# Agent attention with a gated convolution: VectorE subtracts the last low halves, the last chunk is split 384 and 128, and eleven places of TensorE's written order are moved

## The chip, the cores and the metric

The kernel runs on one core of a Trainium2 chip. Its engines work side by side, each through a queue of its own that is done in order: TensorE (PE in the profile) for matrix products, VectorE (DVE), ScalarE (ACT) and GpSimd (POOL) for work on elements, and SyncE (SP), which here issues almost all DMA transfers. The metric is the time of one execution on the device in microseconds (us).

## The reference

Two stages follow each other. Agent attention takes q, k, v of 4 batches x 12800 rows x 128 columns through 49 agents, and its output is the input of a gated convolution with 5 taps:

```python
    a2k = sm(agents, k)
    agent_v = a2k @ v
    q2a = sm(q, agents)
    x = q2a @ agent_v
    for k in range(K):
        gate_pre += conv_w[k][None, None, :] * xp[:, k:k + S, :]
    gate = 1.0 / (1.0 + np.exp(-gate_pre))
    val = x @ w_val
    return (gate * val @ w_out)
```

## The kernel before

**Tiling.** A batch is worked in 10 units of 1280 rows for k, v and q (loads of 640 KB into a ring of 11 slots, `ld`), and in 25 chunks of 512 rows for the gated convolution. A chunk's number t runs over all batches, 0 to 98; the last 512 rows are cut into two chunks, 99 and 100, of 256 rows each (`CUT = 2`). Two units make a segment of 2560 rows, five chunks.

**Stages.** The steps of TensorE have short names, used in the written order and in this document. `k b.u` and `q b.u` are the score products of batch b and unit u (L376), `v b.u` the product of the agents' weights with v (L480), `m` the two small transposes for the maximum of k, `f` the five steps that fold the agents' values with the weights into `stat` and `wo16` (L522 to L728). The softmax of q (the agents' weights for each row) goes over VectorE, GpSimd and ScalarE and ends in a tile `pt`; `t b.u` transposes it into `x1`: by TensorE for the first four units (L849), by a DMA transpose on SP's queue for all others (L835, `x<-pt` in the profile). When both units of a segment have landed, two DMAs copy shifted rows from `x1` into `x2` (L884, `x<-x`), and GpSimd copies a halo of 4 columns for the next segment (L819). Then for each chunk `g t` is the gate's product (five matmuls on `x1`, L922, and a sixth on `x2`, L926), `a t` the value's (L949, L953) and `o t` the output's (L992 to L994).

**A chunk between its products.** ScalarE takes tanh of the gate (`th`), VectorE makes h = (th + 1) * val (L962), ScalarE casts h to f16, the high half `hh` (L968), GpSimd subtracts, `hl` = h - hh (L973), the low half. The output is hh and hl times the folded weights; ScalarE evicts it into `ob` (L1006) and SP sends it out (L1021), two chunks at a time, the last ones of a batch alone.

**What sets the order.** Every step is handed to a planner (`Plan.add`) with the engine, a time in us, and what it reads and writes. TensorE keeps the order in which the steps were written: that is the string `order` in the kernel, with one word for each step. For all other engines and for SP's queue the planner works out an order from the given times: of the steps that could start, it takes the one with the longest work behind it (`Plan.order`). So a word moved in the string, or another time in an `add`, can also move steps on ScalarE, VectorE, GpSimd and SP. Loads are handed over up to 11 ahead of the step that uses them. In the trace, SP waits with whatever stands at the head of its queue, and what is behind it waits too.

Of the kernel before, what the change touches and what calls it, by code (L numbers as in the profile page):

```python
# [13 lines left out]
ALU = mybir.AluOpType  # L14
# [12 lines left out]
CH = 512  # L27
# [12 lines left out]
NT_, NH = 3, 3  # L40
NPT = 4
NX = 4
CUT = 2
NOB = 4
LEAD = 5
MAX_AT = (7, 8)
# [21 lines left out]
class Plan:  # L68
# [11 lines left out]
    def add(self, engine, us, fn, reads=(), writes=(), moved=0.0, key=None, urge=0.0):  # L80
        i = len(self.steps)
        need = set()
        for x in reads:
            need |= self.wrote.get(x, set())
        for x in writes:
            need |= self.wrote.get(x, set()) | self.read.get(x, set())
        for x in reads:
            self.read.setdefault(x, set()).add(i)
        for x in writes:
            self.wrote[x], self.read[x] = {i}, set()  # L90
        self.steps.append((engine, us, fn, need, moved, key))
        self.urge.append(urge)
# [84 lines left out]
def tile_agent_attention_gated_conv(  # L177
# [9 lines left out]
    nc = tc.nc  # L187
    B, C, N = qT.shape
# [3 lines left out]
    NT = B * NCH  # L192
# [56 lines left out]
    def bank():  # L249
# [16 lines left out]
        out=fold, in0=ident[:, 0:AP_], in1=ident[:, AP_:P], op=ALU.add  # L266
# [625 lines left out]


    chunks = [(t // NCH, t % NCH * CH, CH) for t in range(NT - 1)]
    chunks += [(B - 1, N - CH + i * CH // CUT, CH // CUT) for i in range(CUT)]
    banks = {}

    def gates(t):
# [43 lines left out]
    def values(t):  # L942
        b, n0, w = chunks[t]
        stat, x2, o2, xs, x2k, st, th = state.pop(t)
        pv, at_v = banks[t][2:]
        scale = w / CH

        def matmuls():
            nc.tensor.matmul(  # L949
                out=pv, lhsT=stat[:, TAPS, :], rhs=x1s[(b * NCH + n0 // CH) // 5 % NX][:, PAD + o2 : PAD + o2 + w],  # L950
                start=True, stop=False,
            )
            nc.tensor.matmul(  # L953
                out=pv, lhsT=stat[0 : TAPS * X2R, TAPS + 2, :],
                rhs=x2[0 : TAPS * X2R, o2 : o2 + w], start=False, stop=True,
            )

        h, hh, hl = hs[t % NH][:, 0:w], hhs[t % 3][:, 0:w], hls[t % 3][:, 0:w]
        add("pe", 0.43 * scale, matmuls, xs + x2k + st, [at_v], key="c")
        add(  # L960
            "dve", 0.13 + 0.53 * scale,
            lambda: nc.vector.scalar_tensor_tensor(  # L962
                out=h, in0=th, scalar=1.0, in1=pv, op0=ALU.add, op1=ALU.mult
            ),
            [at_v, ("th", t % NT_)], [("h", t % NH)],
        )
        add(
            "act", 0.16 + 0.42 * scale, lambda: nc.scalar.copy(out=hh, in_=h),  # L968
            [("h", t % NH)], [("hh", t % 3)],
        )  # L970
        add(
            "pool", 0.1 + 1.07 * scale,
            lambda: nc.gpsimd.tensor_tensor(out=hl, in0=h, in1=hh, op=ALU.subtract),  # L973
            [("h", t % NH), ("hh", t % 3)], [("hl", t % 3)],
        )

# [80 lines left out]
    for b in range(B):  # L1057
        t0 = b * NCH
# [19 lines left out]
    for t in range(len(chunks) + 2):  # L1078
# [8 lines left out]
    kinds = {"m": "max", "f": "fold"}  # L1087
    order = (
# [25 lines left out]
    )  # L1114
    first = [(kinds.get(x[0], x[0]), *map(int, x[1:].split("."))) for x in order.split()]
    for w in first:
# [5 lines left out]
    def gate_and_state(t):  # L1122
# [3 lines left out]
        "k": key_scores, "v": agent_values, "q": queries, "t": transposes,  # L1126
        "max": lambda b: step(key_max, b), "fold": lambda b: step(fold_weights, b),
        "g": gate_and_state, "a": values, "o": project,
    }
    ahead, done = 0, 0  # L1130
# [56 lines left out]
```

## Time and profile before

| | |
|---|---|
| median of 3 runs (lowest, highest) | 427.45 us (425.69, 428.92) |
| the profiled execution | 425.66 us |
| its span, first to last instruction | 423.6 us |
| mean granted clock of TensorE | 0.985 |
| DMA, all packets | 127.62 MB, mean 301 GB/s |

The times are of one core. The profile is one execution: busy time is what an engine works, and a number in square brackets is the idle time of the engine just before the instruction, with what ended it. In the chain of waits each row is a piece of the chain that ended last, with its start and its length; a DMA's piece runs from its issue to its landing. `PEclk` is the share of full speed that was granted to TensorE's clock, and the DMA share is the busy time of the 16 DMA engines over the stretch, where 1.0 is all of them; it can pass 1.0 because packets of one engine overlap.

### The profile page before, as it was taken

To read this page: it belongs to the slowest core of one execution; us is meant where nothing else is said; L and a number is where in the kernel's file an instruction comes from. 1 tells how busy PE (TensorE), PEld (TensorE's weight loads), DVE (VectorE), ACT (ScalarE), POOL (GpSimd) and SP (SyncE) were. 2 spreads that over 40 slices of the span, in tenths; PEclk is the share of its full clock that TensorE was granted. 3 is DMA by queue.
4 is the path that set the end of the run, shared out by engine and by line. 5 is a ranking of instruction groups with operands and counts; after the bars stand their busy time and mean duration, and the time that the engine had idled before them with its cause. 6 is when DMAs were issued, how large, how long until landed. Compare 5 with 4: busy or idle time off the path is not lost.

```text
span 423.6 us, 10042 instructions
## 1 busy us (share of the span) xinstructions
PE 403.9 (95%) x3907; PEld 197.0 (47%) x3907; DVE 293.3 (69%) x562; ACT 301.5 (71%) x521; POOL 228.2 (54%) x263
## 2 busy tenths in 40 slices
PE   4979999999999999999999899999999989999995
PEld 1358434346555443446555343335555534344443
DVE  3757899867875978667795575767765678676231
ACT  1564568779966777678876486778876567788776
POOL 1002557654657565554566355574366277877553
PEclk9969999999999999999999899999999999999998
DMA  8999999999999999999999999999999977755733
GB/s 320 420 417 411 370 367 353 301 295 310 412 293 283 346 317 362 304 278 356 351 379 324 271 299 370 314 332 302 296 393 322 239 196 161 199 163 176 205 121 124
DMA packets 75129, 127.62 MB, mean 301 GB/s; under 512 B 50466, under 2 KB 50850, under 8 KB 75084
## 3 DMA queue, kind: packets, MB, share of 16 engines
q1 hardware_dynamic: 74940, 126.87, 96.9%
q8 instruction: 30, 0.49, 0.5%
q10 hardware_dynamic: 144, 0.13, 0.2%
q14 instruction: 15, 0.12, 0.1%
HBM read 79.25 MB, written 26.21 MB: 249 GB/s over the span
## 4 chain that ended last, share of the span: by engine, by line
PE 78%; DMA 9%; DVE 8%; ACT 1%; POOL 1%; issue 1%; SPq 0%; POOLq 0%; DVEq 0%; ACTq 0%
PE gate L922 23%; PE sc L376 17%; PE av L480 10%; PE val L949 5%; PE out L992 5%; PE val L953 5%; PE gate L926 5%; PE out L993 4%; DMA ld<-kT 4%; PE out L994 4%; DMA x<-pt 3%; DMA x<-x 2%; DVE h L962 1%; DVE qw L772 1%; DVE qsm L763 1%
## 5 line engine op out<-in xcount | busy, mean ns | idle before, releaser
L973 POOL TENSOR_TENSOR hl<-h,hh 128x512 f16<-128x512 f32 (+1 forms) x101 | 116.9, 1158 | 96.1 <-ACT hh L968 96.0
L922 PE MATMUL gate<-x,stat 128*128 128x512 f16 (+1 forms) x500 | 125.2, 380 | 0.2 <-ACT th L935 0.2
L962 DVE SCALAR_TENSOR_TENSOR h<-th,val 128x512 f32<-128x512 f32 x100 | 67.8, 678 | 66.8 <-PE out L993 26.2
L376 PE MATMUL sc<-ld,ag_sb 128*32 128x320 f32 x1280 | 101.5, 447 | 7.6 <-DMA ld<-kT 7.0
L935 ACT ACTIVATE th<-gate,unscale 128x512 f32<-128x512 f32 x100 | 68.3, 683 | 33.3 <-PE gate L926 31.7
L1006 ACT ACTIVATE ob<-out,oscale 128x512 f32<-128x512 f32 x98 | 67.3, 687 | 21.3 <-PE out L994 20.1
L922 PEld LDWEIGHTS <-stat 128*128 128x128 f16 x505 | 46.3, 97 | 63.7 <-issue 14.8
L968 ACT CAST hh<-h 128x512 f16<-128x512 f32 (+1 forms) x101 | 61.5, 609 | 17.2 <-DVE h L962 16.4
L750 POOL TENSOR_TENSOR qw<-sT,qmx 128x490 f32<-128x490 f32 x40 | 41.4, 1035 | 47.6 <-DVE qmx L745 47.5
L376 PEld LDWEIGHTS sc<-ld,ag_sb 128*32 128x32 f32 x1280 | 36.7, 111 | 59.4 <-issue 25.7
L480 PE MATMUL av<-ld,eT 128*32 128x129 f32 (+1 forms) x1400 | 50.7, 279 | 1.0 <-DVE eT L386 1.0
L480 PEld LDWEIGHTS av<-ld,eT 128*32 128x32 f32 (+1 forms) x1400 | 47.1, 117 | 7.5 <-issue 2.5
L794 POOL TENSOR_TENSOR pt<-qw,pt 128x490 f16<-128x490 f32 x40 | 44.8, 1120 | 3.1 <-ACT pt L779 2.9
L471 ACT ACTIVATE e<-ks,kbias 128x320 f32<-128x320 f32 x80 | 39.3, 554 | 5.4 <-DVE eT L386 3.3
L386 DVE STREAM_TRANSPOSE sT<-sc 128x640 f32<-128x640 f32 x40 | 33.6, 839 | 13.4 <-PE sc L376 12.7
L402 ACT COPY ks<-sc 128x640 f32<-128x640 f32 x40 | 27.7, 691 | 21.2 <-PE sc L376 19.1
L386 DVE STREAM_TRANSPOSE eT<-e 128x640 f32<-128x640 f32 x40 | 33.5, 842 | 9.8 <-ACT e L471 5.2
L926 PE MATMUL gate<-x,stat 95*128 95x512 f16 x100 | 38.3, 383 | 1.5 <-DMA x<-x 1.5
L949 PE MATMUL val<-x,stat 128*128 128x512 f16 x100 | 38.2, 382 | 0.8 <-DVE h L962 0.6
L953 PE MATMUL val<-x,stat 95*128 95x512 f16 x100 | 38.1, 381 | 0.0
L994 PE MATMUL out<-hl,wo 128*128 128x512 f16 x98 | 37.0, 378 | 1.1 <-POOL hl L973 1.1
L992 PE MATMUL out<-hh,wo 128*128 128x512 f16 x98 | 37.3, 381 | 0.1
(130 smaller groups left out, 389.4 us busy)
## 6 DMA issues: line engine op xcount, KB each, us to landing
ld<-kT SPq DMA_DIRECT2D x40, 640.0 KB
ld<-qT SPq DMA_DIRECT2D x40, 640.0 KB
ld<-vP SPq DMA_DIRECT2D x39, 645.0 KB
outT<-ob SPq DMA_DIRECT2D x48, 512.0 KB
x<-x SPq DMA_DIRECT2D x18, 375.0 KB
x<-x SPq DMA_DIRECT2D x18, 100.0 KB
outT<-ob SPq DMA_DIRECT2D x3, 256.0 KB
x<-x SPq DMA_DIRECT2D x4, 187.5 KB
```

Of the source, the lines that this page charges most:

```text
L376: nc.tensor.matmul(out=out[g * BLK : (g + 1) * BLK, j, 0:GT], lhsT=ag_sb[:, b, j * BLK : (j + 1) * BLK], rhs=src[:, g * GT : (g + 1) * GT] ...
L386: nc.vector.transpose(out=out.rearrange("p n (j i) -> p j n i", j=2), in_=in_.rearrange("p j (n i) -> p j n i", i=BLK),)
L480: nc.tensor.matmul(out=av[o + j : o + j + cols, 0 : C + 1], lhsT=et[:, n, j : j + cols], rhs=vt[:, n, :], start=(u == 0 and n < 2), stop=( ...
L922: nc.tensor.matmul(out=pg, lhsT=stat[:, k, :], rhs=x1[:, c : c + w], start=(k == 0), stop=False,)
L926: nc.tensor.matmul(out=pg, lhsT=stat[0 : TAPS * X2R, TAPS + 1, :], rhs=x2[0 : TAPS * X2R, o2 : o2 + w], start=False, stop=True,)
L935: lambda: nc.scalar.activation(out=th, in_=pg, func=AF.Tanh, scale=unscale[:, 0:1]),
L949: nc.tensor.matmul(out=pv, lhsT=stat[:, TAPS, :], rhs=x1s[(b * NCH + n0 // CH) // 5 % NX][:, PAD + o2 : PAD + o2 + w], start=True, stop=False,
L953: nc.tensor.matmul(out=pv, lhsT=stat[0 : TAPS * X2R, TAPS + 2, :], rhs=x2[0 : TAPS * X2R, o2 : o2 + w], start=False, stop=True,)
L962: lambda: nc.vector.scalar_tensor_tensor(out=h, in0=th, scalar=1.0, in1=pv, op0=ALU.add, op1=ALU.mult),
L968: "act", 0.16 + 0.42 * scale, lambda: nc.scalar.copy(out=hh, in_=h),
L973: lambda: nc.gpsimd.tensor_tensor(out=hl, in0=h, in1=hh, op=ALU.subtract),
L1006: lambda: nc.scalar.activation(out=ob[:, o : o + w], in_=po, func=AF.Copy, scale=oscale),
```

## The change

It has three parts. The last 512 rows are cut into 384 and 128 instead of 256 and 256. For the two chunks made of them (t of 99 and 100) the low half is subtracted by VectorE (0.53 us for 512 columns in the planner's table, where GpSimd has 1.07). And in TensorE's written order eleven places are moved: in the first fold the steps `f0`; `q0.6`, `q1.4`, `q2.1` and `q2.8` with `k3.8` to an earlier place, `o44` ahead of the fold `f2`, `k3.2` and `k3.3` behind `o48`, `t2.5` later, `t3.0` earlier, `a72` ahead of `o70`, and in the tail `o96` ahead of `a98`. What is computed stays the same.

```diff
-CUT = 2
+CUTS = (384, 128)
...
-    chunks += [(B - 1, N - CH + i * CH // CUT, CH // CUT) for i in range(CUT)]
+    chunks += [(B - 1, N - sum(CUTS[i:]), w) for i, w in enumerate(CUTS)]
...
-        add(
-            "pool", 0.1 + 1.07 * scale,
-            lambda: nc.gpsimd.tensor_tensor(out=hl, in0=h, in1=hh, op=ALU.subtract),
+        on, eng, us = (nc.vector, "dve", 0.53) if t >= NT - 1 else (nc.gpsimd, "pool", 1.07)
+        add(
+            eng, 0.1 + us * scale,
+            lambda: on.tensor_tensor(out=hl, in0=h, in1=hh, op=ALU.subtract),
...
-        "v0.5 v0.6 v0.7 v0.8 v0.9 f0 t0.0 f0 q0.1 k1.0 f0 k1.1 f0 q0.2 g0 k1.2 f0 t0.1 a0 q0.3 "
+        "v0.5 v0.6 v0.7 v0.8 v0.9 f0 t0.0 q0.1 k1.0 f0 k1.1 f0 f0 q0.2 g0 k1.2 f0 t0.1 a0 q0.3 "
...
-        "o95 g98 a98 o96 g99 o97 a99 g100 a100 o98 o99 o100"
+        "o95 g98 o96 a98 g99 o97 a99 g100 a100 o98 o99 o100"
```

Three queues show what follows from it. The first is SP's, at the transposes of units 1.8 and 1.9 (pt_99 and pt_100), which chunk 45 needs; pt_97 is unit 2.0, x_105 the shifted rows of chunk 45. Before:

```order
L835 DMA_TRANSPOSE x_1_102<-pt_99 128x10x128
L369 DMA ld_71<-kT 128x1280
L835 DMA_TRANSPOSE x_1_102<-pt_100 128x10x128
L1021 DMA outT<-ob_123 128x1024
L369 DMA ld_61<-kT 128x1280
L369 DMA ld_62<-qT 128x1280
L884 DMA x_105<-x_1_102 75x1x2560
```

After:

```order
L835 DMA_TRANSPOSE x_1_102<-pt_99 128x10x128
L369 DMA ld_71<-qT 128x1280
L369 DMA ld_61<-kT 128x1280
L835 DMA_TRANSPOSE x_1_102<-pt_100 128x10x128
L1023 DMA outT<-ob_123 128x1024
L369 DMA ld_62<-kT 128x1280
L835 DMA_TRANSPOSE x_2_103<-pt_97 128x10x128
L884 DMA x_105<-x_1_102 75x1x2560
```

The load of q and one of k now stand ahead of the second transpose, and the transpose of unit 2.0 ahead of the shift.

The second is TensorE's, in the first fold. L564 is the second of its steps `f0`, L659 the third, L376 are score products (of q0.1 on sc_135 and ld_71, k1.0 on ld_61, k1.1 on ld_62), and the row of L849 is the last of `t0.0`. Before:

```order
L849 MATMUL sc_134<-ident_143,pt_97 128x128
L564 MATMUL val<-avT,moe_sb 128x49
L376 MATMUL sc_135<-ld_71,ag_sb 32x320 x8
L376 MATMUL sc_134<-ld_61,ag_sb 32x320 x8
L659 LDWEIGHTS wst_124
```

After:

```order
L849 MATMUL sc_134<-ident_143,pt_97 128x128
L376 MATMUL sc_135<-ld_71,ag_sb 32x320 x8
L376 MATMUL sc_134<-ld_61,ag_sb 32x320 x8
L564 MATMUL val<-avT,moe_sb 128x49
L376 MATMUL sc_135<-ld_62,ag_sb 32x320 x8
L659 LDWEIGHTS wst_124
```

The second step of the fold moved behind two score products, the third behind three.

The third is ScalarE's at the end: casts (hh), tanh (th) and evictions (ob) from chunk 98 on. Before:

```order
L968 CAST hh_116<-h_113 128x512
L935 ACTIVATE th_108<-gate,unscale_131 128x256
L1006 ACTIVATE ob_122<-out,oscale_133 128x512
L968 CAST hh_114<-h_111 128x256
L935 ACTIVATE th_109<-sc_135,unscale_131 128x256
L1006 ACTIVATE ob_122<-sc_134,oscale_133 128x512
L968 CAST hh_115<-h_112 128x256
```

After:

```order
L968 CAST hh_116<-h_113 128x512
L935 ACTIVATE th_108<-gate,unscale_131 128x384
L1008 ACTIVATE ob_122<-out,oscale_133 128x512
L935 ACTIVATE th_109<-sc_135,unscale_131 128x128
L968 CAST hh_114<-h_111 128x384
L968 CAST hh_115<-h_112 128x128
L1008 ACTIVATE ob_122<-sc_134,oscale_133 128x512
```

The tanh of chunk 100 and both casts of the last two chunks moved ahead of the eviction of chunk 98 (ob_122<-sc_134). Behind the last h on VectorE stand two subtractions (128x384 and 128x128) that stood at the end of GpSimd's queue, with 256 columns each.

18 rows, old and new, of the table order are left out of this document.

## The prediction

> **What bounds the kernel now.** I read the page first: who is busy, and when.
>
> ```profile
> PE 403.9 (95%) x3907; PEld 197.0 (47%) x3907; DVE 293.3 (69%) x562; ACT 301.5 (71%) x521; POOL 228.2 (54%) x263
> ...
> DMA  8999999999999999999999999999999977755733
> ```
>
> TensorE is busy for 95% of the span, but the DMA engines stand at 9 up to slice 32 of 40 (some 339 us). So there may be two bounds, one after the other. The table by stretches says where each holds:
>
> ```profile
> core 0: us, PE busy (x), PEclk, DMA share, GB/s
> 200.00:236.00 36.00, 34.51 (x470) 1.00 1.09 337
> 236.00:339.00 103.00, 102.99 (x1031) 0.98 1.09 319
> 339.00:347.00 8.00, 6.31 (x45) 1.00 0.93 213
> 347.00:424.00 77.00, 72.06 (x395) 0.98 0.57 163
> ```
>
> Up to 339 us both are full: the DMA share is 1.09 and TensorE works 102.99 of 103 us. After 347 the share falls to 0.57 and TensorE alone is left. So I next looked at TensorE's timeline for the places behind 200 us where it waits for something:
>
> ```profile
> 235.67 0.39 PE L926 MATMUL gate<-x,stat 95*128 95x512 f16 x1 [1.50 <-DMA x<-x]
> ...
> 340.13 0.38 PE L994 MATMUL out<-hl,wo 128*128 128x512 f16 x1 [1.11 <-POOL hl L973]
> ...
> 346.25 0.38 PE L949 MATMUL val<-x,stat 128*128 128x512 f16 x1 [0.58 <-DVE h L962]
> ```
>
> These are gate 45 (1.50 us), output 69 (1.11) and value 73 (0.58). The chain of waits names what is behind them:
>
> ```profile
> 220.73 7.50 DMA x<-pt
> ...
> 228.28 7.34 DMA x<-x
> ...
> 331.87 6.86 DMA x<-pt
> ...
> 338.78 0.19 POOL x L819
> 338.97 2.23 POOL hl L973 x2
> 341.20 0.57 POOL gw L541
> ...
> 341.79 0.47 DVE wst L607
> ...
> 346.25 0.38 PE val L949
> ```
>
> Gate 45 waits for a shift that lands at 228.28 + 7.34 = 235.62. The other two have one cause: the transpose of unit 3.1 lands at 331.87 + 6.86 = 338.73; GpSimd's halo copy waits for it, and behind that copy stand the low halves of chunks 69 and 70 and the fold's gw, which VectorE needs before its weights and before h of chunk 72. So value 73 at 346.25 hangs on the landing at 338.73, not on when TensorE arrives. TensorE could come 1.11 + 0.58 = 1.69 us later without moving it, and if it came earlier it would wait longer. **The end is the landing of transpose 3.1 plus 346.25 - 338.73 = 7.52 us plus TensorE's work behind value 73.** What is saved ahead of 338 us without making the DMA queue shorter is lost again there. The profiled execution took 425.66 us (span 423.6); the median of the runs is 427.45, so 1.79 is added at the end.
>
> **The change part by part.**
>
> *SP's queue at chunk 45.* The planner has reordered it, as the rows in the part on the change show. One load now stands ahead of transpose 1.9, and transpose 2.0 ahead of the shift. The load was ahead of the shift already; transpose 2.0 is new there.
>
> ```profile
> 212.77 7.23 SPq L835 DMA_TRANSPOSE x<-pt  x1
> ...
> 225.49 0.73 SPq L369 DMA_DIRECT2D ld<-qT  x1
> ...
> 228.28 1.65 SPq L884 DMA_DIRECT2D x<-x  x2
> 230.04 5.71 SPq L835 DMA_TRANSPOSE x<-pt  x2
> ...
> L835 SPq DMA_TRANSPOSE x<-pt x36: 1352/3061/7234, 73.3 to 392.5; - x36
> ```
>
> The trace has no such order, so I bound it. A transpose holds SP for 1.35 us at the least, 3.06 at the median, 7.23 at the most. One load of the queue takes 1.59, the spacing of the first key products, each of which waits for its load:
>
> ```profile
> 18.63 1.28 PE L376 MATMUL sc<-ld,ag_sb 128*32 128x320 f32 x16 [0.30 <-DMA ld<-kT]
> 20.22 1.28 PE L376 MATMUL sc<-ld,ag_sb 128*32 128x320 f32 x16 [0.30 <-DMA ld<-kT]
> ```
>
> With the median, SP comes to transpose 2.0 a load later than it came to q 2.5: 225.49 + 1.59 = 227.1, and is done at 230.1, so the shift is issued 1.9 us later. By the queue alone it lands 1.35 later. I take 1.6, between these two; the ends are 0 (all of it beside loads in flight) and 6.0 (an issue of 7.23). Gate 45 then starts at some 237.3. Those 1.6 us are hidden by the 1.69 us of cover at chunks 69 and 73; of a shift that is later than that, the rest would come through.
>
> *The half clock behind that wait* is there before and after, so it adds nothing here:
>
> ```profile
> 233.57:236.98 3.41, 1.91 (x11) 1.02 (x10) 1.10 (x4) 1.43 (x3) 0.53 (x1) 1.00 1.26 190
> 236.98:240.40 3.42, 3.42 (x9) 1.18 (x9) 2.01 (x7) 1.30 (x2) 1.84 (x3) 0.50 1.05 335
> ```
>
> In the first window TensorE worked 1.91 of 3.41 us, and for the next 3.42 us the granted clock was 0.50, which costs 1.7 us of work. The Trainium skill (TensorE: Matmul & The Clock Gate, section "What's actually happening") wants one idle window of about 3.4 us before the clock is halved; here a wait of 1.50 us was enough, so the measurement decides. By the page's rule the wait of 3.1 us forecast here would leave the clock full and bring TensorE to chunk 69 earlier by 1.7 us, to wait there; the sum is the same, but the slow rival below would be 1.7 us milder.
>
> *The first fold.* On TensorE, f0's second product (L564) now stands behind q0.1 and k1.0, and only k1.1 lies between it and the transposes of the weights (L659).
>
> ```profile
> 42.38 0.42 PE L564 MATMUL val<-avT,moe_sb 128*128 128x49 f32 x2
> ...
> 45.03 0.79 PE L659 MATMUL gate<-ident,wst 128*128 128x128 f16 x8
> ...
> 52.07 0.72 PE L849 MATMUL sc<-ident,pt 128*128 128x128 f16 x10 [0.52 <-DVE sT L386]
> ...
> 43.40 0.20 DVE L588 TENSOR_REDUCE mx<-val 128x1 f32<-128x49 f32 x1
> 44.33 0.53 DVE L582 SCALAR_TENSOR_TENSOR wst<-val,rs,wst 128x30 f16<-128x30 f32 x3
> ```
>
> VectorE's weights run 43.40 to 44.86, 1.46 us; they start some 1.6 us later now (behind sT and qmx of q 0.1), and one product of 1.1 us covers less than two did: up to 0.75 us of new wait ahead of L659. Against it q 0.1's softmax comes earlier and the 0.52 us ahead of L849 goes. Net 0, ends -0.5 to +0.75; either way gate 45 takes it in, where TensorE waits 1.50 us now.
>
> *The other moves* (q0.6, q1.4, q2.1, o44, k3.2, k3.3, t2.5, q2.8, t3.0, a72) lie where the DMA share is 1.09. q2.1, o44 and k3.2 pass steps that TensorE does without a gap, so the same work is done in another order: 0. a72 ahead of o70 brings nothing, since value 73 waits for h of chunk 72, and VectorE's order there is unchanged.
>
> *The queue's length up to transpose 3.1.* SP has the same 217 DMAs ahead of it, before and after. Only SP's holds differ. Shift and transpose 2.1 no longer leave SP 5.71 us in two transposes in a row: a gain of at most 5.71 - 2 x 1.35 = 3.0. Transpose 2.7 moves behind three more DMAs, and while SP then waits for its landing one load instead of three DMAs is queued: a loss of at most 2 x 1.59 = 3.2. I take 0, ends -3.0 and +3.2, which is the widest term.
>
> GpSimd's halo copy waits for transpose 2.7 too, with chunk 60's low half behind it:
>
> ```profile
> 298.82 0.19 POOL L819 COPY x<-x 128x4 f16<-128x4 f16 x1 [2.58 <-DMA x<-pt]
> ...
> 299.94 1.16 POOL L973 TENSOR_TENSOR hl<-h,hh 128x512 f16<-128x512 f32 x1
> ...
> 305.95 0.38 PE L994 MATMUL out<-hl,wo 128*128 128x512 f16 x1
> ```
>
> It comes three DMAs later, at most 3 x 1.59 = 4.8 us, at 303.6, and the low half ends by 303.6 + 0.19 + 1.16 = 305.0; TensorE takes it at 305.95. It is hidden, with 1.0 us of cover; if the landing is later still, TensorE waits there, and chunks 69 and 73 take that in.
>
> *The tail.* On ScalarE both casts of the last chunk now stand ahead of the eviction of chunk 98; before, it stood between them.
>
> ```profile
> 418.24 0.69 ACT L1006 ACTIVATE ob<-sc,oscale 128x512 f32<-128x512 f32 x1
> ...
> 419.23 0.47 ACT L1006 ACTIVATE ob<-sc,oscale 128x256 f32<-128x256 f32 x1
> 419.30 0.67 POOL L973 TENSOR_TENSOR hl<-h,hh 128x256 f16<-128x256 f32 x1 [0.89 <-ACT hh L968]
> ...
> 420.33 0.47 ACT L1006 ACTIVATE ob<-sc,oscale 128x256 f32<-128x256 f32 x1 [0.62 <-PE sc L994]
> ```
>
> The subtract of 0.67 us on GpSimd goes to VectorE, which has nothing else left there; its 128 columns take between 0.53 / 3 = 0.18 us (the 30 columns of the row above) and the 0.67 of 256 columns on GpSimd; I take 0.3. It ends ScalarE's wait of 0.62. ScalarE's work is the same number of columns. Against it, value 98 stands behind output 96, so h of chunk 98 and its cast start later by 0 to 0.6 (beside tanh, or not), of which I take 0.3, and the 384-column piece, the larger one, is sent second last. I take -0.2; the ends are -0.6 (the whole wait) and +0.4.
>
> **Sum.** 425.66 + 0 (fold) + 0 (gate 45: 1.6 hidden) + 0 (queue) - 0.2 (tail) = 425.46; on the median, 427.45 - 0.2 = 427.3.
>
> **The rivals.**
> 1. *TensorE sets the end, not the queue*: then the waits 1.50, 1.7 (clock), 1.11 and 0.58 could all go, 4.9 us, if the moves end them: 427.3 - 4.9 = 422.4. For it: q2.1, o44 and a72 are moved right there. Against: the DMA share of 1.09, and the same 217 DMAs ahead. Chance 0.07.
> 2. *Transpose 2.0 holds SP for 7.23 us ahead of the shift*, as transpose 1.8 did: the shift is 6.0 later, 1.69 of it hidden: +4.3, so 431.6, or 433.3 with a second half-clock window. It decides from an issue of about 7 us; the median of 3.06 speaks against it. Chance 0.08.
> 3. *The queue runs empty while SP waits for transpose 2.7*: transpose 3.1 lands up to 3.2 later, 430.5; about 429.5 is likely then. Against: SP's gain at transpose 2.1. Chance 0.20.
> 4. *The tail does not get shorter*, because the casts ahead of chunk 98's eviction delay the last evictions: +0.4 instead of -0.2, 427.9; it lies within my own case.
>
> **How the numbers follow.** My case has 0.65, with rival 4 in it. A difference of 1% (4.3 us) is about what a measurement of this kernel can tell from no change. Faster by over 1% is rival 1 alone: 0.07. Slower by over 1% is rival 2: 0.08. Within 1% are my case and rival 3: 0.85. The range takes the queue's ends, -3.0 and +3.2, with the tail's: 424.3 to 430.9. Rivals 1 and 2, 0.15, are left outside.
>
> **What would show it.** Right: the DMA share stays above 1 up to 339 us, transpose 3.1 lands at 338 to 340, value 73 starts near 346, gate 45 waits 2 to 4 us, and the waits at output 69 and value 73 shrink. In the tail, ScalarE's 0.62 is gone. Wrong: gate 45 does not wait, and value 73 starts before 343; or transpose 3.1 lands after 342.

## The result and the profile after

The changed kernel takes 430.61 us in the median of 21 runs (427.28 to 432.94), the kernel before 427.26 (423.48 to 430.5) beside it. The ratio is 1.0079, with a 95% interval of 1.0057 to 1.0102: 3.4 us slower. It is small, but it lies outside what the measurement leaves open, and on the other side of the forecast. The ratios are formed from the single runs without the few slow ones (over 1.5% above the fastest of their kernel), so a ratio need not be the quotient of the two medians.

The profiled execution of the changed kernel took 427.28 us (span 425.4). It is the shortest of its 21 runs, so it shows less of the loss than the median: 1.6 us against the profiled execution of before.

The table by stretches, of the changed kernel, answers to the one of before:

```profile
core 0: us, PE busy (x) PEld busy (x) DVE busy (x) ACT busy (x) POOL busy (x), PEclk, DMA share, GB/s
200.00:236.00 36.00, 34.74 (x476) 18.88 (x464) 26.09 (x42) 26.57 (x49) 23.40 (x25) 1.00 1.09 344
236.00:339.00 103.00, 99.64 (x1014) 47.63 (x1015) 71.08 (x133) 73.28 (x127) 54.16 (x60) 0.98 1.06 319
339.00:347.00 8.00, 8.00 (x52) 3.97 (x51) 7.25 (x25) 5.24 (x10) 5.44 (x7) 1.00 0.99 169
347.00:424.00 77.00, 73.65 (x404) 32.03 (x401) 43.05 (x77) 60.00 (x102) 48.51 (x50) 1.00 0.58 174
```

TensorE has lost 3.4 us between 236 and 339 (99.64 busy instead of 102.99), and gained the 1.69 us that it used to wait between 339 and 347. Its timeline names the place (the last bracket is the wait), and the third row is value 73:

```profile
233.50 1.24 PE L922 MATMUL gate<-x,stat 128*128 128x512 f16 x5
239.36 0.48 PE L926 MATMUL gate<-x,stat 95*128 95x512 f16 x1 [4.61 <-DMA x<-x]
...
347.95 0.38 PE L949 MATMUL val<-x,stat 128*128 128x512 f16 x1
```

Gate 45 waits 4.61 us for its shift instead of 1.50, and no wait is left at output 69 and value 73. Value 73 comes at 347.95 instead of 346.25, 1.7 us later, which is the loss of this execution.

The mean DMA share of 236 to 339 us has fallen as well, from 1.09 to 1.06. A narrower stretch shows where, first in the kernel before, then in the changed one:

```profile
300.00:315.00 15.00, 15.00 (x195) 8.14 (x194) 9.75 (x16) 12.06 (x24) 8.22 (x9) 1.00 1.06 352
```

```profile
300.00:315.00 15.00, 15.00 (x169) 7.64 (x161) 11.03 (x16) 13.85 (x27) 8.44 (x9) 1.00 0.93 244
```

For 15 us the DMA engines were not full: 0.93 instead of 1.06, which is 2.0 us of transfer time, and 244 GB/s instead of 352. The window flatters the kernel before in GB/s, since its own wait for transpose 2.7 lies ahead of 300 us (137 GB/s at 296 to 298 us). The stretch of 285 to 315 us holds the place in both, first before, then after:

```profile
285.00:315.00 30.00, 30.00 (x353) 15.40 (x354) 20.92 (x36) 25.43 (x49) 15.26 (x17) 1.00 1.08 319
```

```profile
285.00:315.00 30.00, 30.00 (x314) 14.78 (x315) 22.08 (x36) 26.13 (x48) 16.00 (x17) 1.00 1.00 286
```

That is 1.00 instead of 1.08, 2.4 us of transfer time, and 286 GB/s instead of 319. SP's queue at that place (L835 transpose 2.7, L884 the two shift copies that wait for its landing), before:

```profile
290.88 2.27 SPq L835 DMA_TRANSPOSE x<-pt  x1
293.24 0.54 SPq L1021 DMA_DIRECT2D outT<-ob  x1
293.87 0.54 SPq L369 DMA_DIRECT2D ld<-qT  x1
294.50 0.42 SPq L369 DMA_DIRECT2D ld<-vP  x1
298.78 1.68 SPq L884 DMA_DIRECT2D x<-x  x2
```

and after:

```profile
291.35 0.37 SPq L369 DMA_DIRECT2D ld<-qT  x1
291.81 0.38 SPq L1023 DMA_DIRECT2D outT<-ob  x1
292.28 0.66 SPq L369 DMA_DIRECT2D ld<-vP  x1
293.03 5.57 SPq L835 DMA_TRANSPOSE x<-pt  x1
298.70 0.56 SPq L369 DMA_DIRECT2D ld<-vP  x1
303.40 1.68 SPq L884 DMA_DIRECT2D x<-x  x2
```

Before, three DMAs stand between the transpose and the shift; in the changed kernel one load does. SP stands at the shift until the transpose has landed (298.8 and 303.4) and can issue nothing in that time. What is queued behind the transpose is all that the DMA engines have to do from its landing until the shift's own transfer begins. Short stretches soon after the landing show it, one of the kernel before, then two of the changed kernel:

```profile
300.00:302.00 2.00, 2.00 (x39) 1.10 (x40) 0.99 (x2) 1.63 (x4) 1.38 (x2) 1.00 1.00 414
```

```profile
305.00:307.00 2.00, 2.00 (x80) 2.00 (x76) 1.48 (x2) 2.00 (x6) 1.17 (x1) 1.00 0.75 209
307.00:309.00 2.00, 2.00 (x23) 0.88 (x13) 1.71 (x4) 1.65 (x5) 0.00 (x0) 1.00 0.98 255
```

GpSimd's halo copies start when the transposes of units 2.7 and 3.1 have landed, so they date the landings in the changed kernel:

```profile
303.44 0.19 POOL L819 COPY x<-x 128x4 f16<-128x4 f16 x1 [2.42 <-DMA x<-pt]
...
340.49 0.19 POOL L819 COPY x<-x 128x4 f16<-128x4 f16 x1 [4.18 <-DMA x<-pt]
```

So there were two candidates for the loss: the shift of chunk 45 (theory A below), and a DMA queue that is later up to transpose 3.1 (rival 3 of the prediction, theory D below). In this execution both ends come out alike: gate 45 sets the end, and transpose 3.1 would have set it 0.3 us earlier, at 340.44 + 84.7 = 425.1 (84.7 is what the run e4 below, which waits at output 69 and value 73, has between that landing and its end).

### The profile page after: what moved, and what is told of

Its sections match the earlier page's. It is cut to its first block, busy times and chain, and to the rows that moved or that the text cites. A ratio compares the mean times of both kernels' runs of the same rounds, so it can differ in the third digit from the quotient of the medians.

```text
span 425.4 us, 10035 instructions
## 1 busy us (share of the span) xinstructions
PE 403.5 (95%) x3907; PEld 195.5 (46%) x3907; DVE 297.6 (70%) x564; ACT 300.9 (71%) x521; POOL 227.2 (53%) x261
## 4 chain that ended last, share of the span: by engine, by line
PE 73%; DVE 10%; DMA 10%; ACT 3%; issue 1%; SPq 1%; POOL 1%; ACTq 0%; DVEq 0%; POOLq 0%
PE gate L922 21%; PE sc L376 15%; PE av L480 10%; DMA ld<-kT 5%; PE val L949 5%; PE out L994 4%; PE val L953 4%; PE gate L926 4%; PE out L995 4%; PE out L996 4%; DMA x<-x 3%; DMA x<-pt 2%; DVE kmx L411 1%; DVE h L962 1%; DVE sT L386 1%
## 5 line engine op out<-in xcount | busy, mean ns | idle before, releaser
L975 POOL TENSOR_TENSOR hl<-h,hh 128x512 f16<-128x512 f32 x99 | 116.2, 1175 | 80.8 <-ACT hh L968 77.4
L376 PE MATMUL sc<-ld,ag_sb 128*32 128x320 f32 x1280 | 102.5, 450 | 8.7 <-DMA ld<-kT 8.5
L376 PEld LDWEIGHTS sc<-ld,ag_sb 128*32 128x32 f32 x1280 | 36.6, 112 | 61.2 <-issue 25.4
L480 PE MATMUL av<-ld,eT 128*32 128x129 f32 (+1 forms) x1400 | 49.5, 277 | 0.0
L480 PEld LDWEIGHTS av<-ld,eT 128*32 128x32 f32 (+1 forms) x1400 | 46.0, 115 | 6.7 <-DVE eT L386 1.5
L926 PE MATMUL gate<-x,stat 95*128 95x512 f16 x100 | 38.2, 382 | 4.7 <-DMA x<-x 4.6
L411 DVE TENSOR_REDUCE kmx<-ks 128x2 f32<-128x640 f32 x39 | 31.5, 812 | 9.1 <-ACT ks L402 9.1
```

The lines of the kernel that those rows point to most:

```text
L376: nc.tensor.matmul(out=out[g * BLK : (g + 1) * BLK, j, 0:GT], lhsT=ag_sb[:, b, j * BLK : (j + 1) * BLK], rhs=src[:, g * GT : (g + 1) * GT] ...
L480: nc.tensor.matmul(out=av[o + j : o + j + cols, 0 : C + 1], lhsT=et[:, n, j : j + cols], rhs=vt[:, n, :], start=(u == 0 and n < 2), stop=( ...
L926: nc.tensor.matmul(out=pg, lhsT=stat[0 : TAPS * X2R, TAPS + 1, :], rhs=x2[0 : TAPS * X2R, o2 : o2 + w], start=False, stop=True,)
L975: lambda: on.tensor_tensor(out=hl, in0=h, in1=hh, op=ALU.subtract),
```

## The experiments

All reorder DMAs alone unless said otherwise. DMA steps were given names in the planner (`t2.7` a transpose, `s2.7` the two shift copies it releases, `q3.2` a load), and a list moves them in the planned order, 1 for behind and 0 for ahead. Only the list is shown from e5 on; TensorE, ScalarE, VectorE and GpSimd keep their order. The added lines raise the line numbers a little in these kernels (L821 is L819, L930 is L926). Each time is a median, and each ratio stands against runs of the kernel before on the same chip.

**Is it chunk 45, the tail or the moves?** e1 puts SP's queue at chunk 45 back in the changed kernel:

```diff
-    for i in plan.order():
+    steps = plan.order()
+    for what, where, late in (("t2.0", "s1.9", 1), ("q2.5", "k3.3", 1)):
+        these = [i for i in steps if plan.name.get(i) == what]
+        steps = [i for i in steps if i not in these]
+        at = [n for n, i in enumerate(steps) if plan.name.get(i) == where]
+        n = at[-1] + 1 if late else at[0]
+        steps[n:n] = these
+    for i in steps:
         plan.steps[i][2]()
```

> The changed kernel, with SP's queue at chunk 45 alone put back as before (the load of q 2.5 behind transpose 1.9, transpose 2.0 behind the two shift copies); every other queue as in the changed kernel. Theory A (the shift of chunk 45 is late and only some 1.7 us of lateness is hidden behind it): in the traces the shift lands at 239.31 instead of 235.62, and some 2.1 us of these 3.7 come from this order, the other 1.5 were there already at transpose 1.8. So gate 45 waits 2.0 to 3.0 us here instead of 4.61, and the time falls from 430.6 to 427.5 to 429.0. Rival B (the whole DMA queue is longer, transpose 3.1 lands late whatever stands at chunk 45): within 0.5 us of 430.6. Rival C (the tail or the first fold costs it): 430.6.

It took 431.59 us, 1.0097 (1.0066 to 1.0128): nothing gained. TensorE's timeline shows that the edit did what it should, and where the gain went:

```profile
236.53 0.39 PE L930 MATMUL gate<-x,stat 95*128 95x512 f16 x1 [1.66 <-DMA x<-x]
...
344.53 0.54 PE L1000 MATMUL out<-hl,wo 128*128 128x512 f16 x1 [3.52 <-POOL hl L979]
```

Gate 45 waits 1.66 us instead of 4.61, but output 69 now waits 3.52, since transpose 3.1 landed only at 343.13 (its halo copy starts at 343.18). Theory A as the only cause fell here.

e2 writes the new order of chunk 45 into the kernel before:

```diff
+    for what, where, late in (("t2.0", "s1.9", 0), ("q2.5", "k3.2", 0)):
```

> The kernel before, with SP's queue at chunk 45 alone written as in the changed kernel (the load of q 2.5 ahead of transpose 1.9, transpose 2.0 ahead of the two shift copies). Theory A: the shift lands some 2.1 us later, at 237.7, gate 45 waits 3.6 us, 1.7 of the 2.1 are hidden at chunks 69 and 73: 427.3 + 0.4 to + 1.5, so 427.7 to 428.8. The full 430.6 would say that this order is the whole loss. Rivals B and C: 427.3, no change.

It took 435.36 us, 1.0185 (1.0153 to 1.0216), and tells nothing on the question. In the kernel before, q 2.5 is loaded into the ring slot of q 2.2, so the moved load overwrote it before its score product: unit 2.2 is computed from the rows of unit 2.5 here, and TensorE waited for that load:

```profile
228.66 2.36 PE L378 MATMUL sc<-ld,ag_sb 128*32 128x320 f32 x16 [9.17 <-DMA ld<-qT]
```

e3 is the kernel before with the new tail, e4 with the ten other moves (the words of `order` as in the change, the tail as before):

```diff
+CUTS = (384, 128)
...
-        "o95 g98 a98 o96 g99 o97 a99 g100 a100 o98 o99 o100"
+        "o95 g98 o96 a98 g99 o97 a99 g100 a100 o98 o99 o100"
```

> The kernel before, with the tail of the change alone (384 and 128, the last two low halves on VectorE, output 96 ahead of value 98); SP's queue, ScalarE, VectorE and GpSimd as before up to chunk 98. Theory A and rival B: 427.3 - 0.6 to + 0.2 (the traces of before and of the changed kernel have TensorE's lead shrink by 0.5 us between value 97 and output 99, and grow by 0.3 at output 100). Rival C, tail: 428.5 to 430.6.

> The kernel before, with the ten moves ahead of the tail alone, so all of SP's new order, and the old tail. Theory A and rival B: 430.6 - 0.2 to + 0.6. Rival C, tail: 427.3; rival C, first fold: 430.6, with TensorE behind by the whole loss already at gate 10.

e3 took 426.82 us, 0.9983 (0.9955 to 1.0011). e4 took 430.61, 1.0081 (1.0052 to 1.011): the ten moves are the whole loss, and the tail is none of it. In e4 gate 45 waits 4.57 us and transpose 3.1 lands at 342.74; output 69 and value 73 wait again:

```profile
344.15 0.38 PE L994 MATMUL out<-hl,wo 128*128 128x512 f16 x1 [0.71 <-POOL hl L973]
...
350.27 0.38 PE L949 MATMUL val<-x,stat 128*128 128x512 f16 x1 [0.58 <-DVE h L962]
```

**Transpose 2.7.** e5 puts that place back in the changed kernel but for one output, which stays ahead of the transpose, so that two DMAs stand between it and the shift instead of three; e6 writes the new order into the kernel before, e7 puts this place (as e5 does) and chunk 45 back, and e8 moves transpose 2.0 alone in the kernel before:

```diff
+e5  ("q3.2", "t2.7", 1), ("v3.6", "q3.2", 1), ("v3.7", "s2.7", 1)
+e6  ("t2.7", "v3.6", 1), ("s2.7", "v3.7", 1)
+e7  the three of e5, ("t2.0", "s1.9", 1), ("q2.5", "k3.3", 1)
+e8  ("t2.0", "s1.9", 0)
```

> The changed kernel, with SP's queue at transpose 2.7 alone put back nearly as before: the loads of q 3.2 and v 3.6 stand behind transpose 2.7 and that of v 3.7 behind the two shift copies, instead of ahead of them. Theory D (rival 3 of the prediction: the DMA queue runs thin while SP stands at the shift and waits for transpose 2.7, with a single load queued; transpose 3.1 lands later by that, and the end follows it): the DMA share of 300 to 315 us goes from 0.93 back to 1.03 to 1.07, transpose 2.7 lands near 300, transpose 3.1 1.5 to 3 us earlier than in the run with the old order at chunk 45 (343.1); gate 45 still waits some 4.6 us, so the time falls only as far as that lets it, to 428.5 to 429.5. Theory A (gate 45's lateness alone is the loss): 430.6, no change.

> The kernel before, with the loads of q 3.2, v 3.6 and v 3.7 ahead of transpose 2.7 and its shift, as in the changed kernel; nothing else is moved. Theory D: the DMA share of 300 to 315 us falls from 1.06 to 0.86 to 0.95, transpose 3.1 lands 1.5 to 3 us later than 338.7 and the time is 428.5 to 430. Theory A: 427, no change.

> The changed kernel with both places of SP's queue put back, that at chunk 45 and that at transpose 2.7. If A and D together are the loss (each hidden while the other stands), the time is 427.0 +- 0.7, that of before, or 0.5 below it by the tail. If it stays above 429, a third place costs it (the queue at 80 to 110 us, where SP's order is also new).

> The kernel before, with transpose 2.0 alone ahead of the two shift copies of chunk 45, as in the changed kernel; no load is moved. Theory A: the shift lands some 1.5 to 3.5 us later than 235.6, gate 45 waits 3 to 5 us, 1.7 of that is hidden at chunks 69 and 73: 427 + 0 to + 1.8. Theory D: 427 + 0 to + 0.5.

e5 took 429.55 us, 1.0062 (1.0031 to 1.0093); e6 429.8, 1.0069 (1.004 to 1.0098); e7 429.28, 1.0045 (1.0015 to 1.0075); e8 428.41, 1.0011 (0.998 to 1.0042). e6 settles it from the side of before: two loads and an output moved ahead of one transpose, and a load ahead of the shift that waits for it, cost 0.69%, nearly the whole loss. Its profile has the thin stretch of the changed kernel (259 GB/s), and transpose 3.1 as late:

```profile
300.00:315.00 15.00, 15.00 (x173) 7.67 (x165) 10.49 (x16) 13.32 (x26) 7.14 (x9) 1.00 1.03 259
```

```profile
343.05 0.19 POOL L821 COPY x<-x 128x4 f16<-128x4 f16 x1 [6.62 <-DMA x<-pt]
```

Part of that lateness is older than the edit: in this execution gate 45 waits 3.78 us with a queue that is up to there the one of before, and the halo copy behind transpose 2.5 starts at 284.37 instead of 280.86. From that copy to the one behind transpose 3.1 it takes 58.7 us, against 57.9 in before and 56.6 in e3. So the 0.69% rests on the median of twelve runs, and the trace agrees with it in direction. The share of 1.03 missed its forecast of 0.86 to 0.95. The share counts the time of packets, also while they move little (1.26 with 137 GB/s at 296 to 298 us in the kernel before); the GB/s have to be read beside it. e8's ratio can't be told from 1, so transpose 2.0 ahead of the shift is not shown to cost anything by itself; up to 1.8 us is left open (its profiled execution, at 430.8 us, is a late one, where gate 45 waits 4.69 us). The changed kernel does not come back as readily: e5's interval still takes in its 1.0079, and e7 lies above its forecast of 427.0 +- 0.7.

**A third place, the start, and whether transpose 3.1 sets the end.** e9 puts transpose 2.8 back as well. e10 is the kernel before with the moves of `f0` and q0.6 in `order`. e11 and e12 are new orders of the kernel before:

```diff
+e9  those of e7, ("v3.8", "t2.8", 1), ("v3.9", "v3.8", 1), ("q3.3", "v3.9", 1), ("q3.4", "q3.3", 1), ("q3.5", "q3.4", 1)
+e11 ("q3.8", "t3.1", 1), ("q3.9", "q3.8", 1)
+e12 those of e11, ("k3.3", "s1.9", 1), ("q2.5", "k3.3", 1)
```

> The changed kernel with three places of SP's queue put back: that at chunk 45, that at transpose 2.7, and transpose 2.8, which stands ahead of the five loads from v 3.8 to q 3.5 again instead of behind them. If transpose 2.8's place is what the run with two places put back still lacks: 427.0 +- 0.7, and the DMA share of 300 to 315 us at 1.05 or more. If the rest comes from the start (SP's order at 80 to 110 us): 429, as with two places.

> The kernel before, with the moves of the first fold and of q 0.6 alone, which bring SP's new order at 50 to 110 us with them. If the rest of the loss comes from there: 428.3 to 429. If not: 426.8 +- 0.6, since what TensorE gains or loses ahead of gate 45 ends in its waits, and transpose 3.1 lands as before.

> The kernel before, with the loads of q 3.8 and q 3.9 behind transposes 3.0 and 3.1 on SP's queue instead of ahead of them; nothing else is moved. If the landing of transpose 3.1 sets the end: it lands some 3.2 us earlier (two loads of 1.59), and the end comes earlier until TensorE has no wait left at output 69 and value 73, 1.7 us in the profile of before: 425.0 to 425.8. If TensorE sets the end by itself, or the two loads are then late for their score products: 427 or more.

> As the run before, and the two shift copies of chunk 45 also ahead of the loads of k 3.3 and q 2.5. The shift then lands 2 to 3 us earlier, gate 45 no longer waits (1.5 us, and the half clock of 1.7 us behind it goes), and transpose 3.1's early landing lets it come through: 423 to 424.5. If the landing of transpose 3.1 did not set the end, the gate's wait alone would give 0 to 1.5 us.

e9 took 428.44 us, 1.0029 (1.0004 to 1.0055): most of the loss is gone, though it too missed 427.0 +- 0.7, and e5, e7 and e9 can't be told from each other, so what each place gives back is not shown. e10 took 426.99, 1.0004 (0.9972 to 1.0036): the first fold costs nothing. e11 took 425.47, 0.9962 (0.9938 to 0.9986): two loads behind transposes 3.0 and 3.1 make the kernel faster by 1.6 us, about the 1.69 that TensorE waited at output 69 and value 73; neither waits in its profile, and the halo copy is at

```profile
337.82 0.19 POOL L821 COPY x<-x 128x4 f16<-128x4 f16 x1 [3.47 <-DMA x<-pt]
```

e12 missed by far: 429.64 us, 1.0048 (1.0016 to 1.008), some 3.7 us slower than e11 by the ratios. SP's queue at chunk 45 in e12 (the shift waits for transpose 1.9, issued at 223.28):

```profile
223.28 2.63 SPq L837 DMA_TRANSPOSE x<-pt  x1
226.00 1.45 SPq L1025 DMA_DIRECT2D outT<-ob  x1
230.81 1.66 SPq L887 DMA_DIRECT2D x<-x  x2
232.57 1.10 SPq L370 DMA_DIRECT2D ld<-kT  x1
```

Gate 45 does not wait here, but its last product starts no earlier than in e11 (237.03 and 237.05). One output is all that is queued behind the transpose while SP stands; from 226 to 234 us the DMA engines move 242 GB/s, against 379 in e11. Transpose 3.1 lands 4.9 us later than in e11, at 342.67. It is the pattern of transpose 2.7 at another place.

**Late, or run dry?** e13 leaves transpose 2.7 as late as the change has it and puts three DMAs behind it. e14 leaves it as early as before and puts one there. e15 moves two loads in between transposes 1.8, 1.9 and the shift of chunk 45. e16 is e11 with the new tail:

```diff
+e13 ("s2.7", "v3.8", 1)
+e14 ("v3.6", "s2.7", 1), ("q3.2", "s2.7", 1)
+e15 those of e11, ("k3.0", "t1.9", 1), ("k3.1", "k3.0", 1)
+e16 those of e11, with the tail of e3
```

> The changed kernel; transpose 2.7 stays where the change has it, but three DMAs (the load of v 3.7, an output, the load of v 3.8) stand between it and the shift it releases, where the change leaves one. If the queue ran dry there: the DMA share of 300 to 315 us goes from 0.93 to 1.0 or more, transpose 3.1 lands 1 to 2.5 us earlier than without it, and the time falls from 430.6 to 428.5 to 429.6, as with transpose 2.7 put back. If transpose 2.7's own lateness costs it: 430.6 or more, since the shift is then later still.

> The kernel before; transpose 2.7 stays where it was, but the loads of q 3.2 and v 3.6 stand behind the shift it releases, so that one output alone is queued while SP waits for its landing, where there were three DMAs. If a queue that runs dry costs the time: the DMA share of 295 to 310 us falls below 1, transpose 3.1 lands 2 to 4 us later, and the time is 429 to 431. If transpose 2.7's lateness is what costs: 427, no change.

> The kernel before, with q 3.8 and q 3.9 behind transposes 3.0 and 3.1 (425.5 in its own run), and the loads of k 3.0 and k 3.1 behind transposes 1.8 and 1.9, so that both transposes are two loads earlier and four DMAs, two of them these loads, are queued ahead of the shift of chunk 45. The shift lands 2 to 3 us earlier without running the queue dry, gate 45's wait of 1.5 us and the half clock behind it go: 422.5 to 424. If transpose 1.8 waits for its own data there, SP stands and the queue runs dry: 426 or more.

> The kernel before, with q 3.8 and q 3.9 behind transposes 3.0 and 3.1, and the tail of the change (384 and 128, the last low halves on VectorE). If the two add up: 425.5 - 0.7 to + 0, so 424.8 to 425.5.

e13 took 428.77 us, 1.0039 (1.0016 to 1.0062), e14 430.14, 1.0084 (1.0051 to 1.0118). Their stretches of 300 to 315 us, e13 first:

```profile
300.00:315.00 15.00, 15.00 (x220) 8.71 (x211) 12.05 (x18) 14.34 (x28) 7.82 (x8) 1.00 1.07 329
```

```profile
300.00:315.00 15.00, 15.00 (x192) 8.16 (x194) 9.66 (x16) 13.19 (x25) 8.82 (x10) 1.00 0.91 269
```

and the halo copies of e14, behind transposes 2.7 and 3.1:

```profile
301.37 0.19 POOL L821 COPY x<-x 128x4 f16<-128x4 f16 x1 [3.25 <-DMA x<-pt]
...
343.88 0.19 POOL L821 COPY x<-x 128x4 f16<-128x4 f16 x1 [9.18 <-DMA x<-pt]
```

In e13 transpose 2.7 lands at 305.11, later than in the changed kernel, and about half of the loss is gone all the same. In e14 it lands as it does in e3, whose queue is that of before (the halo copies start at 301.37 and 301.48), and the whole loss is there; no product of TensorE waits for a load in e14 behind 295 us. From the copy behind transpose 2.5 to the one behind 3.1 it takes 60.4 us in e14 and 56.6 in e3. So the number of DMAs queued behind the transpose sets the loss there, not when the transpose lands. In three pairs of kernels, one DMA there instead of three costs 0.69% (e6), 0.84% (e14) and, from e11 to e12, 0.86 points; e5, e7 and e9 have two.

e15 took 424.0 us, 0.9932 (0.9902 to 0.9962), e16 424.26, 0.9944 (0.9914 to 0.9974); both beat both kernels, and neither can be told from e11. That gate 45's wait goes, as e15 was to show, its profile does not bear out: with five DMAs between transpose 1.9 and the shift, the shift lands 11.1 us after its issue, at 239.17 (7.3 in before), and gate 45 waits 4.05 us. But this is the slowest of e15's twelve runs, and in the profile of e17 below, the fastest of its twelve and with the same queue at this place, gate 45 does not wait. What the two loads give there stays open.

e17 adds the new tail to e15, and e18 has the eleven moves with nearly the same order of DMAs at the five places (as in e5, two DMAs stand behind transpose 2.7 instead of three):

```diff
+e17 those of e15, with the tail of e3
+e18 the changed kernel with those of e9 and of e15
```

> The kernel before with all that has helped: q 3.8 and q 3.9 behind transposes 3.0 and 3.1, k 3.0 and k 3.1 behind transposes 1.8 and 1.9, and the tail of the change. If they add up: 424.0 - 0.7 to + 0, so 423.3 to 424.0, faster than both kernels.

> The changed kernel with its three places put back (chunk 45, transposes 2.7 and 2.8) and the same two moves of loads as in e17, so the eleven moves of TensorE's order with a well fed queue. If the moves themselves cost nothing and the landing of transpose 3.1 was all of the loss: as e17, 423.3 to 424.3. If they cost what the run with three places put back still lacked: 1.0 to 1.5 more than e17.

e17 took 425.15 us, 0.9948 (0.992 to 0.9976): faster than both kernels, but the gains do not add up; e15, e16 and e17 can't be told from each other. e18 took 426.9, 1.0015 (0.9988 to 1.0041), so the moves, the missing third DMA behind transpose 2.7, or SP's order at the places that were not put back still cost some 1.75 us against e17. Which of them it is was not tried.

## Why the prediction was wrong

- **What sets the end: held.** "The end is the landing of transpose 3.1", plus a fixed rest: in e3 to e8 and e10, where TensorE waits at output 69 and value 73, 84.6 to 84.9 us lie between that landing and the end, as in before (423.6 - 338.73 = 84.9), while the landing itself runs from 339.60 to 343.26. In e1, e9 and e14 the wait at output 69 is over 3 us and the rest is longer, 85.4 to 85.7. e11 brought it forward on purpose and gained.
- **The queue's length up to transpose 3.1: the step that failed.** It was set to 0, "the same 217 DMAs", with ends of -3.0 and +3.2. e6 alone measures +3.0 (429.8 - 426.81), close to the upper end, and e14 +3.4 (430.14 - 426.75). The count is the same in both traces and did not matter: what mattered is how many DMAs stand between a transpose and the shift that waits for it. The loss was in sight in the same sentence ("while SP then waits for its landing one load instead of three DMAs is queued"), and was set off against a gain at transpose 2.1 that did not come: transposes 2.0 and 2.1 hold SP for 3.32 and 3.19 us in the changed kernel, 6.5 together, where they held it for 5.71. Rival 3, with a chance of 0.20 and some 429.5 us, was the case that came. It is the mechanism that was given the weight 0 here; the range still holds 430.6 only because its upper end was built from it.
- **Gate 45: right in kind, too small.** The shift was put 1.6 us later, "hidden by the 1.69 us of cover". It landed 3.7 later in the profiled execution (239.31 against 235.62); there the cover was used up and 1.7 came through. One pair of executions does not size it, since the wait differs from one to the next: with the old order of this place gate 45 waits 1.14 to 3.78 us (before, e1, e3, e6, e7, e9, e10, e11, e14, e16), with transpose 2.0 ahead of the shift 4.57 to 4.69 (after, e4, e5, e8, e13). The 1.50 us that the forecast started from lie at the low end. e1 shows that this alone was not the loss of the median.
- **Rivals 1 and 2: fell.** TensorE gained nothing from the moved words, and transpose 2.0 held SP for 3.32 us, not 7.23; e8 has it at 1.0011.
- **The first fold, 0: held** (e10, 1.0004). **The halo copy at chunk 60, 303.6: held** (303.44, without a wait at output 60 in the changed kernel; in e1, where it came at 305.9, TensorE waited 2.4 us there).
- **The tail, -0.2: not told from nothing.** e3 gives -0.7 us (-1.9 to +0.5). ScalarE's wait of 0.62 us is gone, as was forecast.
- **The other moves, 0: open**, with e18's 1.75 us against it.
- **The signs named were too coarse.** "The DMA share stays above 1 up to 339 us" holds for the mean (1.06), and hides 15 us at 0.93. Transpose 3.1 lands at 340.44 in the changed kernel's profile, between the signs for right and for wrong; in e4, nearer its median, it lands at 342.74.

## What to carry to other kernels

Where one queue issues all transfers in order, and an entry waits for a landing, count the DMAs between the transfer that lands and the entry that waits for it: in these traces they are all that keeps the DMA engines busy meanwhile. Here one instead of three cost 0.7 to 0.9%, and bringing the waiting entry (e12's shift) forward by taking loads from ahead of it made things worse. When a planner reorders a full queue, the number of its entries need not show the loss, and did not here; look at each place where the queue's head stands still, and at the share and the GB/s in stretches of a few us around it; one stretch of 15 us can catch the place in one kernel and miss it in the other.

## What was not expected of the hardware

Whether TensorE's clock is halved behind a wait at gate 45 does not follow from the wait's length. Waits of 1.49 (e9), 1.66 (e1) and 2.90 us (e10) left it at 1.00; behind waits of 1.50 (before), 2.67 (e7) and 4.61 us (after) it was 0.50 for some 3 us. e16 waits 2.90 us as e10 does, and there the clock is at 0.50 from 239.5 to 242.9 us. The stretch of 239 to 242 us in e10, then in e7, whose gates 45 start 0.3 us apart, has granted clocks of 1.00 and 0.51:

```profile
239.00:242.00 3.00, 3.00 (x28) 1.55 (x30) 2.70 (x11) 2.25 (x4) 1.85 (x3) 1.00 1.02 303
```

```profile
239.00:242.00 3.00, 3.00 (x12) 1.34 (x11) 2.68 (x8) 1.19 (x2) 1.85 (x3) 0.51 1.07 318
```

The Trainium skill (TensorE: Matmul & The Clock Gate, section "What's actually happening") says that the window over which the clock gate measures runs freely and does not start with the kernel; that would fit waits of nearly the same place and length with different outcomes. Its rule that one idle window of some 3.4 us comes first does not fit the waits of 1.50 and 2.67 us that halved the clock, which are shorter than that.
